# First phase of a packed-attention mixer: keys turned by TensorE, scores and packed values in small tiles

## The chip, the cores and the metric

The kernel runs on one core of one Trainium2 chip. The metric is the device time of one execution in microseconds. A core has five engines that run side by side, each strictly in the order of its own instructions: TensorE (PE, matrix products and turns by a product with the identity), VectorE (DVE), ScalarE (ACT), GpSimd (POOL) and SyncE (SP), which issues all the transfers of this kernel. They wait for each other by semaphores. Data lie in the SBUF memory with 128 partitions; TensorE writes into PSUM, which has eight banks of 512 fp32 columns; ACT and DVE bring results from there into SBUF.

## What is computed

Two attentions follow one another, then a mixer over tokens and channels. q, k and v are 8 x 8 x 576 x 64 (batch, head, token, head dimension), p is 8 x 8 x 32 x 64.

```python
def sm_attn(qq, kk, vv):
    s = scale * np.matmul(qq, kk.transpose(0, 1, 3, 2))
    s = s - np.max(s, axis=-1, keepdims=True)
    a = np.exp(s)
    a = a / (np.sum(a, axis=-1, keepdims=True) + 1e-09)
    return np.matmul(a, vv)
p_packed = sm_attn(p, k, v)
out = sm_attn(q, p_packed, p_packed)
...
xt = x.transpose(0, 2, 1)
h = xt @ U @ V
u = x + h.transpose(0, 2, 1)
ch = np.maximum(u @ w_ch1, 0.0) @ w_ch2
return (u + ch).astype(np.float32)
```

x is the attention's output with its heads side by side, 8 x 576 x 512. U, V, w_ch1 (512 x 2048) and w_ch2 (2048 x 512) come as 64-bit floats, and the kernel makes fp32 of their bits. Because the packed attention's result has only 32 rows a head, the kernel multiplies p_packed with w_ch1 first ("pp w1" below, the folds) and uses that product as weights later.

## The kernel before

**First phase (the loop `for i in range(NU + 3)`, lines 479 to 508).** A unit is one batch and four of its heads; there are 16. For each unit the keys come as rows (`load_nat`, line 97: 18 tokens of one head to a partition, 4.6 KB in one run), DVE turns them by 32x32 blocks into `kT` (`transposed`, line 101). p is scaled by GpSimd and turned by DVE into block-diagonal tiles `bdp` (lines 310 and 313). The scores of four heads are four fp32 products of 128x128 by 288 columns into one tile `s_ps` of two PSUM banks (line 322). Softmax takes a maximum on DVE (line 330) and an exponential with running sum on ACT (line 332). The weights are turned back by TensorE (lines 342 and 343; ACT copies them out at 345 and 346), and the packed values are five products of all four heads at once (lines 358 and 359), 256 columns wide, of which each head's 32 rows use their own 64 columns; ACT scales these four blocks into `ppall` (line 362). Values come as two transfers a unit (lines 300 and 302).

Beside it in the same loop: conversions of w1 from 64-bit bits (`some_w1`: ACT line 67, four DVE instructions at 68 to 71, a split by ACT 123 and GpSimd 124), the folds (`fold`: three products a piece at 76 to 78 into `w_ps`, copied out at 390 or 392, stored to `wsr`), the pairs (`a_pairs`) and the steps of `attention(0)`, 16 small functions, one popped in each turn from i = 5.

The order of the first phase is not written out by hand: a planner simulates the engines in time, with the program's order as priority, and fixes each engine's order and each buffer's reuse. The eight PSUM banks in this phase are two for `psT` (tag t), two for `s_ps`, one for `pp_ps` and three for `w_ps`.

**The large loop** (from the first `h_ps` product at lines 76 to 78 on) runs over 8 batches with 16 pieces each, in an order written out by hand (`manual_schedule`). It needs the packed result of the first batch's attention, the folds of the first two batches and the first pieces of w2.

Of the kernel before, what the change touches and what calls it, by code (L numbers as in the profile page):

```python
# [19 lines left out]
def packed_attention_mixer_kernel(  # L20
# [36 lines left out]
    HALF = ((0, 256), (256, 320))  # L57

# [71 lines left out]
    def load_uv(pool):  # L130
        bits = pool.tile([P, NB * D], F32, name="nat", bufs=3)
# [5 lines left out]
        vbits = pool.tile([P, NB * D], F32, name="nat", bufs=3).bitcast(I32)  # L137
# [143 lines left out]
    bdp = [sA.tile([P, 4, P], F32, name=f"bdp{i}", tag=f"bdp{i}", bufs=1) for i in range(2)]  # L281
# [4 lines left out]
    ua = {}  # L286

    def a_load(u):
        b, g = UN[u]
        ua[u] = {}  # L290
        if g == 0:
            ua[u]["p"] = sA.tile([P, 2, D], F32, name="pn")
            nc.sync.dma_start(out=ua[u]["p"], in_=p[b].rearrange("(g h) n d -> (h n) g d", g=2))
        ua[u]["nat"] = load_nat(sA, 3, k, b, g)

    def a_load_v(u):
        b, g = UN[u]
        gh = slice(4 * g, 4 * g + 4)
        vt = pipe.tile([P, 5, 4 * D], F32, name="vt", tag="vt", bufs=2)
        nc.sync.dma_start(out=vt[:, :4].rearrange("p h x -> p (h x)").rearrange("p (h x) -> p h x", h=4),  # L300
                          in_=v[b, gh, :SM].rearrange("h (p k) d -> p h (k d)", k=4))
        nc.sync.dma_start(out=vt[:64, 4].rearrange("p (h d) -> p h d", h=4),
                          in_=v[b, gh, SM:].rearrange("h p d -> p h d"))
        ua[u]["v"] = vt

    def a_split(u):
        b, g = UN[u]
        if g == 0:
            pn = ua[u]["p"]
            nc.gpsimd.tensor_scalar_mul(pn, pn, scale)  # L310
            for h in range(4):
                hs = slice(32 * h, 32 * h + 32)
                nc.vector.transpose(bdp[b % 2][hs, :, hs], pn[hs].rearrange("p g (e l) -> p (g e) l", l=32))  # L313
        ua[u]["kT"] = transposed(sA.tile([P, 2, S], F32, name="kT"), ua[u]["nat"])

    def a_scores(u):
        b, g = UN[u]
        kT = ua[u]["kT"]
        s_ps = psA.tile([P, 2, 512], F32, name="s_ps", bufs=1)
        for hf in range(2):  # L320
            for dh in range(2):
                nc.tensor.matmul(s_ps[:, hf, :288], lhsT=bdp[b % 2][:, 2 * g + dh], rhs=kT[:, dh, 288 * hf:288 * hf + 288],  # L322
                                 start=dh == 0, stop=dh == 1)
        ua[u]["s"] = s_ps

    def a_softmax(u):
        s = ua[u]["s"][:, :, :288]
        mx = sA.tile([P, 1], F32, name="mx")
        sm = sA.tile([P, 1], F32, name="sm", bufs=3)
        nc.vector.tensor_reduce(mx, s, axis=AX.XY, op=ALU.max, negate=True)  # L330
        e1 = sA.tile([P, 2, 288], F32, name="e1")
        nc.scalar.activation(e1, s, AF.Exp, bias=mx, accum_out=sm)
        ua[u]["e"] = e1.rearrange("p a x -> p (a x)")
        ua[u]["sum"] = sm

    def a_turn(u):
        e1 = ua[u]["e"]
        t_ps = psT.tile([P, 4, P], F32, name="t_ps", tag="t")
        t2_ps = psT.tile([P, 512], F32, name="t2_ps", tag="t")
        e1c = e1[:, :SM].rearrange("p (j k) -> p k j", k=4)  # L340
        for kk in range(4):
            nc.tensor.transpose(t_ps[:, kk], e1c[:, kk], ident)
        nc.tensor.transpose(t2_ps[:64, :P], e1[:, SM:], ident)
        eT = sA.tile([P, 5, P], F32, name="eT", bufs=2)
        nc.scalar.copy(eT[:, :4], t_ps)
        nc.scalar.copy(eT[:64, 4], t2_ps[:64, :P])
        ua[u]["eT"] = eT
        sm = ua[u]["sum"]
        nc.vector.tensor_scalar_add(sm, sm, 1e-9)
        nc.vector.reciprocal(sm, sm)  # L350

    def a_pack(u):
        b, g = UN[u]
        eT, vt, rs = ua[u]["eT"], ua[u]["v"], ua[u]["sum"]
        pp_ps = psA.tile([P, 4, D], F32, name="pp_ps", bufs=1)
        vm = vt[:, :4].rearrange("p h x -> p (h x)").rearrange("p (h k d) -> p k h d", h=4, k=4)
        for kk in range(4):
            nc.tensor.matmul(pp_ps, lhsT=eT[:, kk], rhs=vm[:, kk], start=kk == 0, stop=False)
        nc.tensor.matmul(pp_ps, lhsT=eT[:64, 4], rhs=vt[:64, 4].rearrange("p (h d) -> p h d", h=4), start=False, stop=True)
        for h in range(4):  # L360
            hs = slice(32 * h, 32 * h + 32)
            nc.scalar.activation(ppall[hs, b, g], pp_ps[hs, h], AF.Copy, scale=rs[hs])
        if b < B // 2:
            ua[u]["twice"] = sA.tile([P, 2, D], F32, name="twice", bufs=1)
            nc.scalar.copy(ua[u]["twice"], ppall[:, b, g].unsqueeze(1).to_broadcast([P, 2, D]))
# [91 lines left out]
    for t in bdp:  # L457
        nc.gpsimd.memset(t, 0.0)
# [326 lines left out]
```

## Time and profile before

| what | value |
|---|---|
| time, three runs: median (lowest to highest) | 871.32 us (870.49 to 874.37) |
| profiled execution, its own time | 876.01 us |
| its span in the trace | 874.2 us |
| TensorE busy in the span | 826.7 us (95%) |
| VectorE | 512.6 us (59%) |
| ScalarE | 374.0 us (43%) |
| GpSimd | 258.6 us (30%) |

The trace shows one execution. TensorE's busy time counts products that lie over one another in the pipeline as busy until their modelled end, so a full stretch isn't necessarily at peak. fp32 products show as two records each, those in fp32r as one. The granted clock is the share of its full speed that TensorE had.

### The profile page before, as it was taken

What the parts mean: (1) busy time and instruction counts of PE and PEld (TensorE: products, weight loads), DVE (VectorE), ACT (ScalarE), POOL (GpSimd) and SP (SyncE); (2) the same over time, 40 slices, a digit from 0 to 9 for tenths busy, and PEclk for the clock granted to TensorE, in tenths of its full rate; (3) what the DMA queues carried; (4) which work ended last, traced back from release to release, by engine and by line L of the source; (5) the groups of instructions that cost most, each with busy time, mean ns of one, the idle gap of its engine ahead of it and who ended that gap; (6) DMA issues with size and microseconds to landing.
All of it is one profiled execution on the core that took longest, in us unless ns stands there. A gap on an engine that the chain in (4) does not pass through costs nothing.

```text
span 874.2 us, 12574 instructions
## 1 busy us (share of the span) xinstructions
PE 826.7 (95%) x4440; PEld 706.8 (81%) x4440; DVE 512.6 (59%) x1032; ACT 374.0 (43%) x960; POOL 258.6 (30%) x230
## 2 busy tenths in 40 slices
PE   4779889988989999999999999999999999999997
PEld 2557666777879888888888888988888889889886
DVE  7999985889857876478676433443543424432220
ACT  2557576534445554455554332233333322333220
POOL 3302353545343313132233232323242313221110
PEclk9989997999999999999999999999999999999999
DMA  9869775723424444334453103010301120002001
GB/s 318 236 204 330 221 222 187 253 85 121 160 64 123 140 144 130 98 112 126 117 182 85 53 13 112 25 60 17 112 25 63 56 70 25 25 14 95 25 1 60
DMA packets 59998, 98.55 MB, mean 113 GB/s; under 512 B 12192, under 2 KB 36768, under 8 KB 59936
## 3 DMA queue, kind: packets, MB, share of 16 engines
q1 hardware_dynamic: 59936, 97.75, 36.0%
q8 instruction: 35, 0.57, 0.3%
q14 instruction: 27, 0.22, 0.1%
HBM read 71.52 MB, written 26.21 MB: 112 GB/s over the span
## 4 chain that ended last, share of the span: by engine, by line
PE 73%; DVE 17%; DMA 4%; ACT 3%; issue 3%; SPq 0%; POOL 0%; DVEq 0%; ACTq 0%; POOLq 0%
PE o L78 14%; PE o L77 14%; PE o L76 14%; PE h_ps L76 7%; PE h_ps L77 7%; PE h_ps L78 7%; DVE kT L101 3%; DVE os L70 2%; DVE natT L101 2%; DVE os L69 2%; DMA bits<-in_moe_w_ch_dram 2%; PE w_ps L592 2%; DVE os L71 2%; DVE os L68 2%; PE s_ps L322 2%
## 5 line engine op out<-in xcount | busy, mean ns | idle before, releaser
L640 DVE SCALAR_TENSOR_TENSOR hl<-h_ps,hh 128x256 fp32r<-128x256 f32 x256 | 104.1, 418 | 181.1 <-ACT hh L638 145.7
L78 PE MATMUL o<-w2h,hl 128*128 128x512 f32 x512 | 202.1, 395 | 0.0
L76 PE MATMUL o<-w2h,hh 128*128 128x512 f32 x512 | 201.3, 393 | 0.0
L77 PE MATMUL o<-w2l,hh 128*128 128x512 f32 x512 | 200.9, 392 | 0.0
L638 ACT ACTIVATE hh<-h_ps 128x256 fp32r<-128x256 f32 x256 | 96.0, 383 | 234.4 <-PE h_ps L78 231.4
L76 PE MATMUL h_ps<-ah,fold 128*128 128x256 f32 x496 | 149.3, 301 | 6.3 <-DVE hl L640 5.9
L453 POOL TENSOR_TENSOR fold<-fold 128x512 fp32r<-128x512 f32 x62 | 81.2, 1310 | 230.1 <-ACT fold L452 222.6
L77 PE MATMUL h_ps<-al,fold 128*128 128x256 f32 x496 | 146.1, 295 | 0.0
L78 PE MATMUL h_ps<-ah,fold 128*128 128x256 f32 x496 | 145.7, 294 | 0.0
L78 PEld LDWEIGHTS o<-w2h,hl 128*128 128x128 f32 x512 | 96.4, 188 | 21.6
L77 PEld LDWEIGHTS o<-w2l,hh 128*128 128x128 f32 x512 | 96.6, 189 | 17.5
L76 PEld LDWEIGHTS o<-w2h,hh 128*128 128x128 f32 x512 | 96.7, 189 | 16.8
L76 PEld LDWEIGHTS h_ps<-ah,fold 128*128 128x128 f32 x496 | 93.5, 188 | 13.4 <-DVE hl L640 10.3
L77 PEld LDWEIGHTS h_ps<-al,fold 128*128 128x128 f32 x496 | 93.5, 189 | 2.1
L78 PEld LDWEIGHTS h_ps<-ah,fold 128*128 128x128 f32 x496 | 93.3, 188 | 0.0
L181 POOL TENSOR_TENSOR nlo<-natT,nhi 128x576 fp32r<-128x576 f32 x32 | 46.0, 1453 | 115.5 <-ACT nhi L180 115.5
L68 DVE TENSOR_SCALAR os<-os 128x512 f32<-128x512 f32 (+2 forms) x51 | 37.1, 727 | 40.0 <-ACT os L67 39.9
L322 PE MATMUL s_ps<-kT,bdp 128*128 128x288 f32 x128 | 39.3, 457 | 9.4 <-DVE bdp L313 9.2
L180 ACT CAST nhi<-natT 128x576 fp32r<-128x576 f32 x32 | 20.7, 675 | 55.8 <-DVE natT L101 48.6
L124 POOL TENSOR_TENSOR w1l<-os,w1h 128x512 fp32r<-128x512 f32 x16 | 21.4, 1337 | 67.7 <-ACT w1h L123 61.1
L101 DVE STREAM_TRANSPOSE kT<-nat 128x1152 f32<-128x1152 f32 x16 | 37.3, 2329 | 5.7 <-DMA nat<-in_k_dram 5.6
L67 ACT ACTIVATE os<-bits 128x512 f32<-128x512 f32 x48 | 32.3, 674 | 18.9 <-DMA bits<-in_moe_w_ch_dram 14.7
(143 smaller groups left out, 1398.5 us busy)
## 6 DMA issues: line engine op xcount, KB each, us to landing
bits<-in_moe_w_ch_dram SPq DMA_DIRECT2D x48, 512.0 KB, 4.3
nat<-in_k_dram SPq DMA_DIRECT2D x16, 576.0 KB, 5.3
nat<-in_q_dram SPq DMA_DIRECT2D x16, 576.0 KB, 4.4
vt<-in_v_dram SPq DMA_DIRECT2D x16, 512.0 KB, 5.6
wsr<-fold SPq DMA_DIRECT2D x32, 256.0 KB, 3.8
out_dram<-bits SPq DMA_DIRECT2D x16, 512.0 KB, 3.0
wsc<-bits SPq DMA_DIRECT2D x64, 128.0 KB, 2.2
fold<-wsc SPq DMA_DIRECT2D x32, 256.0 KB, 2.8
```

The costliest lines, as they stand in the source:

```text
L67: nc.scalar.activation(t, high.bitcast(F32), AF.Abs)
L68: nc.vector.tensor_single_scalar(t, t, LEAST, op=ALU.max)
L76: nc.tensor.matmul(ps, lhsT=lh, rhs=rh, start=start, stop=False)
L77: nc.tensor.matmul(ps, lhsT=lh, rhs=rl, start=False, stop=False)
L78: nc.tensor.matmul(ps, lhsT=ll, rhs=rh, start=False, stop=stop)
L101: nc.vector.transpose(t.rearrange("p h (i c) -> p c h i", c=NB), nat.rearrange("p (c h l) -> p c h l", h=2, l=32),)
L124: nc.gpsimd.tensor_tensor(lo, x, hi.bitcast(F32), op=ALU.subtract)
L181: nc.gpsimd.tensor_tensor(lo[:, dh], t, hi[:, dh].bitcast(F32), op=ALU.subtract)
L322: nc.tensor.matmul(s_ps[:, hf, :288], lhsT=bdp[b % 2][:, 2 * g + dh], rhs=kT[:, dh, 288 * hf:288 * hf + 288], start=dh == 0, stop=dh == 1)
L453: nc.gpsimd.tensor_tensor(lo, raw, hi.bitcast(F32), op=ALU.subtract)
L638: nc.scalar.activation(hi, src, AF.Relu)
L640: nc.vector.scalar_tensor_tensor(lo, src, 0.0, hi.bitcast(F32), op0=ALU.max, op1=ALU.subtract)
```

## The change

Only the first phase is changed. Keys are loaded with nine tokens to a partition (two runs of 2.3 KB, two heads side by side), turned by TensorE in blocks of two tokens and copied out of PSUM by ACT and DVE, so that the head dimension of even tokens lies in partitions 0 to 63 and that of odd ones in 64 to 127. p is loaded twice side by side and turned by TensorE. The scores are eight products a unit with 64 rows and 32 columns of the array, into two banks, one for each half of the tokens. Softmax works on the two halves. Packed values are 20 products a unit with 32 columns of the array and 64 columns of data, without the blocks that were computed and not used; one ACT instruction scales them. Values come in five transfers a unit. The six PSUM banks of the phase are now three pairs, with tags k (turned keys, p, weights turned back and packed values), s and w. In the loop, w1's conversions and the steps of `attention(0)` come earlier, the latter two in a turn.

```diff
+    NT = 9
+    I = S // NT
+    KHALF = (slice(0, 5 * I), slice(5 * I, S))
+    KLAST = slice(4 * I, 5 * I)
...
-    psA = actx.enter_context(tc.tile_pool(name="psA", bufs=1, space=PSUM, reuse_waits="tile"))
+    psA = actx.enter_context(tc.tile_pool(name="psA", bufs=2, space=PSUM, reuse_waits="tile"))
...
+    def bank(tag):
+        return psA.tile([P, 512], F32, name=f"{tag}_ps", tag=tag)
...
+            pn[b] = sA.tile([P, 2, 2, D], F32, name="pn", bufs=1)
+            for z in range(2):
+                nc.sync.dma_start(out=pn[b][:, :, z], in_=p[b].rearrange("(g h) n d -> (h n) g d", g=2))
+        ua[u]["x"] = sA.tile([P, 2 * S], F32, name="kx", bufs=3)
+        nc.sync.dma_start(
+            out=ua[u]["x"].rearrange("p (h y) -> p h y", h=2),
+            in_=k[b, 4 * g:4 * g + 4].rearrange("(h z) (i c) d -> (z i) h (c d)", z=2, c=NT))
...
+        for h in range(4):
+            nc.sync.dma_start(out=vt[:, h], in_=main[h].rearrange("i (a x) -> i a x", a=2))
+        nc.sync.dma_start(out=vt[:64, 4].rearrange("p (h d) -> p h d", h=4), in_=rows[:, 8])
+
+    def a_p(b):
+        t_ps = bank("k")
+        pT[b] = sA.tile([P, 2, P], F32, name="pT")
+        for i in range(2):
+            nc.tensor.transpose(t_ps[:, P * i:P * i + P], pn[b][:, i].rearrange("p z d -> p (z d)"), ident)
+        nc.scalar.activation(pT[b].rearrange("p g n -> p (g n)"), t_ps[:, :2 * P], AF.Copy, scale=scale)
+
+    def a_turn(u):
...
+        t = ua[u]["t"] = sA.tile([P, 4, 5 * I], F32, name="kT")
+        x = ua[u]["x"].rearrange("p (h y) -> p h y", h=2)
+        for h in range(2):
+            t_ps = bank("k")
+            for j in range(4):
+                o = P * (2 * (j % 2) + j // 2)
+                nc.tensor.transpose(t_ps[:, o:o + P], x[:, h, P * j:P * j + P], ident)
+            src = t_ps.rearrange("p (k a z i) -> p a z k i", k=2, a=2, z=2)
+            for a in range(2):
+                dst = t[:, 2 * h:2 * h + 2, :4 * I].rearrange("p z (k i a) -> p z k i a", k=2, a=2)[:, :, :, :, a]
+                if a:
+                    nc.vector.tensor_copy(dst, src[:, a])
+                else:
+                    nc.scalar.copy(dst, src[:, a])
+        t_ps = bank("k")
+        for h in range(2):
+            nc.tensor.transpose(t_ps[:64, P * h:P * h + P], x[:, h, SM:], ident)
+        nc.scalar.copy(t[:64, :, KLAST], t_ps[:64, :2 * P].rearrange("p (h i) -> p h i", h=4))
+
+    def a_scores(u):
...
+        ss = [bank("s") for _ in range(2)]
+        for h in range(4):
+            hs = slice(32 * h, 32 * h + 32)
+            for r in range(2):
+                rs = slice(64 * r, 64 * r + 64)
+                n = KHALF[r].stop - KHALF[r].start
+                nc.tensor.matmul(ss[r][hs, :n], lhsT=lT[rs, g, hs], rhs=t[rs, h, :n], start=True, stop=True)
...
+        for r in range(2):
+            nc.vector.tensor_reduce(mx[:, r:r + 1], ss[r], axis=AX.X, op=ALU.max, negate=True)
+        nc.vector.tensor_tensor(mx[:, 2:], mx[:, :1], mx[:, 1:2], op=ALU.min)
+        e1 = ua[u]["e"] = sA.tile([P, S], F32, name="e1")
+        for r in range(2):
+            nc.scalar.activation(e1[:, KHALF[r]], ss[r], AF.Exp, bias=mx[:, 2:], accum_out=sm[:, r:r + 1])
+
+    def a_turn_back(u):
...
+        t_ps = bank("k")
+        for kk in range(4):
+            c0 = 5 * I * (kk % 2) + P * (kk // 2)
+            nc.tensor.transpose(t_ps[:, P * kk:P * kk + P], e1[:, c0:c0 + P], ident)
+        nc.scalar.copy(eT[:, :4].rearrange("p k x -> p (k x)"), t_ps)
+        t_ps = bank("k")
+        nc.tensor.transpose(t_ps[:64, :P], e1[:, KLAST], ident)
+        nc.vector.tensor_copy(eT[:64, 4], t_ps[:64, :P])
...
     def a_pack(u):
...
+        p_ps = bank("k")
+        vk = vt[:, :4].rearrange("p h x -> p (h x)").rearrange("p (h k d) -> p k h d", h=4, k=4)
+        for kk in range(5):
+            rows = P if kk < 4 else I
             for h in range(4):
                 hs = slice(32 * h, 32 * h + 32)
...
+                rhs = vk[:, kk, h] if kk < 4 else vt[:rows, 4, D * h:D * h + D]
+                nc.tensor.matmul(p_ps[hs, :D], lhsT=eT[:rows, kk, hs], rhs=rhs, start=kk == 0, stop=kk == 4)
         if b < B // 2:
...
+            nc.scalar.activation(ua[u]["twice"], p_ps[:, :D].unsqueeze(1).to_broadcast([P, 2, D]), AF.Copy, scale=ua[u]["rs"])
+            nc.gpsimd.tensor_copy(ppall[:, b, g], ua[u]["twice"][:, 0])
+        else:
+            nc.scalar.activation(ppall[:, b, g], p_ps[:, :D], AF.Copy, scale=ua[u]["rs"])
...
-            w_ps = psA.tile([P, 512], F32, name="w_ps", bufs=3)
+            w_ps = bank("w")
...
-            a_turn(i - 1)
+            a_turn_back(i - 1)
...
-        if i + 1 < NU:
-            a_split(i + 1)
+            a_turn(i + 1)
...
-        if i > 1:
+        if i > 0:
             some_w1()
...
-        if i >= 5 and first and i not in (16, 17):
-            first.pop(0)()
+        for _ in range(2):
+            if i >= 4 and first:
+                first.pop(0)()
...
-        if 6 < i < 13:
+        if 5 < i < 12:
             some_w1()
+        if i == 2:
+            uv = load_uv(sA)
         if i == 3:
-            uv = load_uv(sA)
-        if i == 4:
             prepare_uv(*uv)
```

More of the change, by code (lines that the diff above doesn't have):

```diff
@@ L130, in load_uv @@
     def load_uv(pool):
-        bits = pool.tile([P, NB * D], F32, name="nat", bufs=3)
+        bits = pool.tile([P, NB * D], F32, name="kx", bufs=3)
         ub = bits[:, :10 * R].bitcast(I32)
@@ new lines, in a_scores @@
+    def a_scores(u):
+        b, g = UN[u]
+        t, lT = ua[u]["t"], pT[b]
+        ss = [bank("s") for _ in range(2)]
[5 more added lines that the diff above has]
+                nc.tensor.matmul(ss[r][hs, :n], lhsT=lT[rs, g, hs], rhs=t[rs, h, :n], start=True, stop=True)
+        ua[u]["s"] = [ss[r][:, :KHALF[r].stop - KHALF[r].start] for r in range(2)]
@@ L316, in a_scores @@
[L316 to L350, printed above, removed]
```

53 lines of the change are left out of this document (20 added, 33 removed).

## The prediction

> **What bounds the kernel now.** I read three views first: the table of busy time by stretch, the engines' timeline for the ends of the first phase, and the chain of waits of that phase. The first timeline rows are the first scores, the last scores and the first product of the large loop.
>
> ```profile
> 9.16 4.18 PE L322 MATMUL s_ps<-kT,bdp 128*128 128x288 f32 x8 [9.16 <-DVE bdp L313]
> ...
> 120.72 2.11 PE L322 MATMUL s_ps<-kT,bdp 128*128 128x288 f32 x8
> ...
> 162.62 0.28 PE L76 MATMUL h_ps<-ah,wt 128*128 128x256 f32 x1
> ```
>
> The first phase therefore ends at 162.6 us: 9.2 us of start, then 16 units at a pace of (120.7 - 9.2) / 15 = 7.4 us, then 42 us from the last scores to the large loop. What follows it, 874.2 - 162.6 = 711.6 us, holds none of the changed code, and I leave it as it is. The question is only where the 162.6 goes.
>
> ```profile
> core 0: us, PE busy (x) PEld busy (x) DVE busy (x) ACT busy (x) POOL busy (x), PEclk, DMA share, GB/s
> 0.00:20.00 20.00, 8.40 (x29) 6.05 (x29) 14.11 (x22) 5.35 (x9) 8.42 (x18) 1.00 0.93 310
> 20.00:40.00 20.00, 14.24 (x65) 10.14 (x63) 19.50 (x35) 11.30 (x31) 6.63 (x7) 1.00 0.81 241
> 40.00:60.00 20.00, 14.60 (x47) 10.46 (x46) 18.76 (x42) 9.39 (x26) 1.16 (x2) 0.74 0.69 211
> 60.00:80.00 20.00, 19.88 (x91) 15.25 (x91) 19.09 (x34) 14.55 (x40) 4.34 (x4) 1.00 0.95 299
> 80.00:100.00 20.00, 17.64 (x80) 12.98 (x79) 19.50 (x32) 13.49 (x37) 6.83 (x5) 1.00 0.83 268
> 100.00:120.00 20.00, 18.14 (x78) 13.48 (x76) 18.64 (x37) 12.68 (x31) 7.54 (x6) 0.91 0.71 213
> 120.00:140.00 20.00, 16.59 (x60) 11.94 (x60) 11.66 (x22) 14.11 (x34) 9.46 (x7) 0.75 0.65 204
> 140.00:160.00 20.00, 17.45 (x74) 11.85 (x74) 14.46 (x24) 12.55 (x27) 10.24 (x11) 0.99 0.70 218
> ```
>
> Three stages are to be seen. Up to 60 us **VectorE (DVE)** is full, 38.3 of the last 40 us, while TensorE (PE) idles. From 60 to 120 us **both** are nearly full: DVE 57.2 and PE 55.7 of 60 us. After 120 us neither is, and transfers and conversions follow one another. So a microsecond taken from DVE is worth a microsecond only up to 60 us; after that PE is right behind it, and this change moves work onto PE.
>
> The chain of waits prices PE's work by what really passes between instructions (the busy times of PE overlap). It is a stretch in which PE is never idle:
>
> ```profile
> 62.93 1.94 PE s_ps L322 x8
> 64.87 1.73 PE pp_ps L358 x8
> 66.60 0.47 PE t_ps L342 x4
> 67.07 0.63 PE pp_ps L359 x2
> 67.70 0.43 PE w_ps L76
> 68.13 0.23 PE w_ps L77
> ...
> 70.53 0.11 PE t_ps L343
> ```
>
> An fp32 product of the program is two passes in the trace (four calls, eight records in `s_ps`): 1.94 / 8 = 0.242 us for 288 columns, 0.84 ns a column and pass. A turn of a 128x128 block costs 0.117 us. The product with 64 rows costs 0.315 a pass against 0.216 for those with 128 rows, and the one after it 0.43 against 0.23: entering and leaving 64 rows cost some 0.2 us each. A unit now takes PE 1.94 + 1.73 + 0.63 + 0.47 + 0.11 + 0.2 = **5.1 us**.
>
> **The change part by part.** DVE first, by these groups of the first 165 us:
>
> ```profile
> L101 DVE STREAM_TRANSPOSE kT<-nat 128x1152 f32<-128x1152 f32 x16 | 37.3, 2329 | 5.7 <-DMA nat<-in_k_dram 5.6
> L390 DVE COPY fold<-w_ps 128x512 f32<-128x512 f32 x8 | 5.5, 683 | 2.3 <-DMA wsr<-fold 2.3
> L362 ACT ACTIVATE ppall<-pp_ps,sm 32x64 f32<-32x64 f32 x64 | 19.5, 304 | 7.8 <-PE pp_ps L359 7.1
> L330 DVE TENSOR_REDUCE mx<-s_ps 128x1 f32<-128x576 f32 x16 | 12.0, 747 | 0.3
> L332 ACT ACTIVATE e<-s_ps,mx 128x576 f32<-128x576 f32 x16 | 11.8, 739 | 12.1 <-DVE mx L330 11.9
> L313 DVE STREAM_TRANSPOSE bdp<-pn 32x128 f32<-32x128 f32 x32 | 9.5, 295 | 0.4
> L346 ACT COPY eT<-t_ps 64x128 f32<-64x128 f32 x16 | 4.1, 257 | 0.7 <-PE t_ps L343 0.7
> L349 DVE TENSOR_SCALAR sm<-sm 128x1 f32<-128x1 f32 x16 | 2.3, 144 | 0.6 <-ACT e L332 0.5
> L332 ACT ACTIVATION_READ_ACCUMULATOR e<-s_ps,mx 128x1 f32 x16 | 3.1, 193 | 0.0
> L239 ACT CAST ms<-m_ps 128x256 fp32r<-128x256 f32 x1 | 0.4, 365 | 0.0
> ```
>
> It loses the turn of the keys and the block transposes of p: 37.3 + 9.5 = 46.8 us. It gains, per unit, two copies of 128x256 out of PSUM (half of the 683 ns row and a little: 0.37 each), the small copy of the turned weights (0.26, as ScalarE (ACT) needs for it now), one more maximum and a minimum (about 0.2: one more start and a one-column instruction of 0.14). That is 16 x 1.2 = 19 us, so DVE drops by **27 us**, from 135.7 us over these eight stretches to 109. At the fullness of the first 120 us (109.6 of 120 busy, 91%) that is 120 us of time: DVE no longer sets the phase.
>
> ACT gains two copies of 128x256 and the last token's, 3 x 0.365, a share of p's turn 0.19, the split of the exponential (one more start and accumulator read, 0.35), and loses the small copy 0.26 and four scalings, 1.22, for one of 0.3. Net +0.5 us a unit, 7 us in all on an engine that is busy 93 of 160: hidden behind the others. GpSimd loses the scaling of p and gains eight small copies: off the path.
>
> PE is the uncertain term. Turning keys adds 10 turns of 0.117 and half of p's two: 1.3 us. The way back keeps its 0.58. Entering and leaving 64 rows now happens twice a unit (scores and the last tile of values), four times 0.2 = 0.8.
>
> The scores become 8 calls of two passes with 320 or 256 columns, 0.27 and 0.215 us a pass. Nothing in this trace shows what tiles of 64x32 or 128x32 do side by side. One end is strictly in turn: 4 x 2 x (0.27 + 0.215) = 3.9 us. The other end is all eight tiles together: 0.54. I take the nearest mechanism: the two passes of a call use one tile and must follow each other, and records start in order, so only the second pass of a call lies beside the first of the next. That gives half, 1.94 + 0.2 = **2.1 us**, about today's.
>
> The values become 20 calls, 40 passes of 64 columns, each 0.054 us and each with a weight load. In turn at the streaming rate: 2.15. In pairs: 1.1. All four tiles of a column together: 0.54. If each pass costs the 0.11 us that the closest records of small products have now: 4.4. I take **1.6**, midway between pairs and in turn, since 40 loads must also get through. A unit: 1.3 + 2.1 + 0.6 + 1.6 + 0.8 = **6.4 us** against 5.1. The rest of PE's work in the phase is 96 passes of the folds at 0.23 = 22 us and about 7 us of attention(0) and pairs: 29. New PE work 16 x 6.4 + 29 = 131 us. At the 94% that PE reaches from 60 to 100 us (37.5 of 40) this is 140 us, plus 9 us of start, plus 2 for the end: the large loop would start at **151 us**, 11.6 us earlier. The time for that lost at half clock (granted 0.74 and 0.75 in two stretches) goes with PE's idle gaps, and I count no gain beyond.
>
> The Trainium skill, "TensorE: Matmul & The Clock Gate", Part 3, says that tiles in distinct row and column groups run beside each other, the later ones starting some 4 ns apart. No run here shows it. By it the scores and values would cost about 0.6 us each, which is the first rival below. "TensorEngine Tiling (Array Packing)", Key Properties, says that a change of the tiling mode drains TensorE. The 0.2 us at 64 rows agrees with it; the product with 64 columns, 0.11 us, shows no such price.
>
> The loads: k arrives as two runs a partition in place of one, p twice, v in five transfers in place of two.
>
> ```profile
> 120.14 0.38 SPq L300 DMA_DIRECT2D vt<-in_v_dram  x1
> 120.57 0.61 SPq L302 DMA_DIRECT2D vt<-in_v_dram  x1
> ...
> wsr<-fold SPq DMA_DIRECT2D x32, 256.0 KB, 3.8
> ```
>
> SyncE's (SP) issues grow by 3 x 0.38 + 0.2 for p, 1.3 us a unit of some 7: no bound. The bytes grow only by p's second copy, 0.5 MB at about 300 GB/s = 2 us spread over the phase. It shows only if the DMA share of 0.95 (60 to 80 us) holds everywhere.
>
> The moved steps are the conversions of w1 and the steps of attention(0), two a unit from unit 4. They add no work; they fill the stretch after the last scores (42 us now, with DVE 26 of 40 busy) earlier. That is what lets PE's sum set the phase at all; if they don't move, up to 10 us of the gain stays there.
>
> **The rivals.**
>
> 1. *Full overlap of tiles.* Scores 0.6 and values 0.6: a unit 3.9 us, PE 91 us in all. Then DVE's 120 us, 6 us of start and some 14 for the last folds, their store (3.8 us to land) and their reload decide: 140 us, 22 us gained, **849 us**. For it speaks that no two of the eight score tiles share rows and columns; against it that both passes of a call share one.
>
> 2. *Tiles in turn: PE becomes the bound, slower than before.* Place: scores and values. Price: 3.9 + 2.15 + 2.7 = 8.7 us a unit, 168 us of PE, 179 at 94%, 188 with the start: 25 us lost, **896 us**; with 0.11 a pass, 10.9 us a unit and about 935. It decides from the unit at which (16 x + 29) / 0.94 + 9 = 162.6: x = **7.2 us**. My 6.4 is not far from that. The stretch from 60 to 120 us, with PE at 93%, speaks for it.
>
> 3. *The two k banks.* Six and a half fills a unit (three for keys, two back, one for values, half for p) go through two banks. If the mean time from first write to last read is c, a unit needs 3.25 c; it decides from c = 7.4 / 3.25 = 2.3 us. Fill and eviction alone are 0.47 + 0.58, about 1.1, so 3.6 us a unit. But ACT now comes late: in one unit the bank was filled from 118.85 and its copy ended at 122.14, 3.3 us.
>
> ```profile
> 118.85 0.63 PE L342 MATMUL t_ps<-ident,e 128*128 128x128 f32 x4
> ...
> 121.57 0.57 ACT L345 COPY eT<-t_ps 128x512 f32<-128x512 f32 x1
> ```
>
> At 2.7 us, midway between 2.3 and that, the pace is 8.8 and the phase 15 x 1.4 = 21 us longer, less some 10 for the shorter end: 11 lost, **882 us**. Against it: other work (scores, folds, attention) has other banks and can stand between.
>
> 4. *Nothing gained.* PE units at 7 us, or the steps don't move forward: within 4 us, **871 us**.
>
> **How the numbers follow.** The profiled execution took 876.0 us, 1.8 outside its span; the median of three is 871.3. I set the gain against the median: 871.3 - 11.6 = 860, rounded up to **861** for p's bytes. Chances: forecast (a gain of 5 to 18) 0.37, full overlap 0.20, nothing gained 0.15, tiles in turn 0.15, k banks 0.13. About 0.5% (4.4 us) is what a measurement can tell: faster 0.57, same 0.15, slower 0.28. The range leaves one in ten on each side: from 838 (full overlap, with a shorter end too) to 892 (most of the way to tiles in turn). The likeliest case by itself is 853 to 867.
>
> **What would show it.** PE's timeline of one unit after: scores near 2.1 us and values near 1.6 confirm the pairs; 0.6 each, rival 1; 3.9 and 2.2 or more, rival 2. Groups: DVE down by 25 to 29 us in the first 150. Idle of PE before the key turns, released by ACT or DVE copies out of the k banks, beyond 1 us a unit shows rival 3. The first product of the large loop near 151 us. I am wrong if the part after it changes by more than 4 us, or if the first unit starts later than 12 us because of the added loads.

## The result, and the profile after

The kernel after took **897.2 us** (median of four runs, 896.12 to 899.77) against 872.85 us for the kernel before in the same session: **1.028 times as long [1.024, 1.032]**, so it is slower, outside the predicted range and on the other side. The forecast was 861.

The timeline of TensorE (start, duration, engine, line, operation, tiles) answers first. These are the first scores, one unit in the middle (values, then scores), the last scores and the first product of the large loop.

```profile
9.77 1.31 PE L361 MATMUL s_ps<-kT,pT 64*32 64x320 f32 x16
...
117.74 0.90 PE L400 MATMUL k_ps<-vt,eT 128*32 128x64 f32 x40
119.16 0.76 PE L361 MATMUL s_ps<-kT,pT 64*32 64x320 f32 x16
...
162.22 0.76 PE L361 MATMUL s_ps<-kT,pT 64*32 64x320 f32 x16
181.81 0.56 PE L82 MATMUL h_ps<-ah,wt 128*128 128x256 f32 x1
```

The large loop starts at 181.8 us in place of 162.6: 19.2 of the 21.6 us by which the span grew (895.8 against 874.2). What follows took 895.8 - 181.8 = 714.0 us against 711.6. Within the phase the pace is (162.2 - 9.8) / 15 = 10.2 us a unit in place of 7.4, while the stretch from the last scores to the loop shrank from 41.9 to 19.6 us. Yet TensorE's price of a unit fell far below the forecast: scores 0.76 us, values 0.90.

The table by stretch shows that no engine fills the phase as a whole any more; VectorE alone is full, and only from 40 to 80 us (37.2 of 40 us). After the first two columns (stretch, length) stand the busy times of TensorE, its weight loads, VectorE, ScalarE and GpSimd, then the granted clock.

```profile
core 0: us, PE busy (x) PEld busy (x) DVE busy (x) ACT busy (x) POOL busy (x), PEclk, DMA share, GB/s
0.00:20.00 20.00, 10.99 (x60) 5.38 (x61) 8.23 (x20) 7.88 (x17) 5.56 (x13) 1.00 0.85 275
20.00:40.00 20.00, 11.25 (x105) 6.00 (x104) 15.93 (x36) 9.05 (x25) 4.60 (x5) 0.72 0.75 252
40.00:60.00 20.00, 12.24 (x102) 7.63 (x106) 18.09 (x43) 10.91 (x31) 5.75 (x5) 0.50 0.65 193
60.00:80.00 20.00, 16.11 (x177) 10.58 (x169) 19.10 (x41) 12.62 (x30) 9.54 (x9) 0.93 0.83 250
80.00:100.00 20.00, 15.00 (x160) 9.40 (x160) 15.75 (x34) 14.23 (x37) 10.44 (x10) 0.83 0.96 306
100.00:120.00 20.00, 15.80 (x167) 8.96 (x168) 11.76 (x33) 13.54 (x37) 6.50 (x7) 0.91 0.82 233
120.00:140.00 20.00, 15.63 (x168) 10.50 (x169) 7.84 (x22) 9.28 (x25) 0.00 (x0) 0.78 0.97 281
140.00:160.00 20.00, 18.29 (x192) 12.76 (x192) 11.93 (x35) 11.79 (x37) 3.15 (x4) 0.96 0.44 131
```

VectorE's eight rows add up to 108.6 us, where 109 was forecast, but the phase isn't over at 160 us now. TensorE, which was to set the phase at 94%, is busy for 11 to 16 of 20 us in most rows. It waits, and one unit shows for what:

```profile
65.01 0.66 PE L338 MATMUL k_ps<-ident,kx 128*128 128x128 f32 x4 [0.34 <-DVE eT L385]
66.17 0.66 PE L338 MATMUL k_ps<-ident,kx 128*128 128x128 f32 x4 [0.50 <-ACT pT L325]
67.48 0.39 ACT L345 COPY kT<-k_ps 128x256 f32<-128x256 f32 x1
68.20 0.40 ACT L345 COPY kT<-k_ps 128x256 f32<-128x256 f32 x1
69.30 0.42 DVE L343 COPY kT<-k_ps 128x256 f32<-128x256 f32 x1
69.78 0.41 PE L348 MATMUL k_ps<-ident,kx 128*64 128x128 f32 x2 [1.04 <-DVE kT L343]
70.75 0.41 DVE L343 COPY kT<-k_ps 128x256 f32<-128x256 f32 x1
```

The first key bank is filled from 65.01; ScalarE copies its half out at 67.48, VectorE the other half only at 69.30. Both banks with tag k are taken by then, so the turn of the last token (L348) and everything behind it in TensorE's order stand until 69.78. The bank was held for 69.72 - 65.01 = 4.71 us, the second for 71.16 - 66.17 = 4.99.

In this unit no idle time stands before VectorE's copies: it is at other work when ScalarE's copy ends. But that it comes second is no chance. In all 32 banks of the trace its copy starts after ScalarE's of the same bank has ended, and the groups of the first 182 us (line, operation, count, busy, mean; idle time before them and what ended it) show it waiting for that in other units:

```profile
L338 PE MATMUL k_ps<-ident,kx 128*128 128x128 f32 x128 | 25.6, 345 | 12.2 <-ACT pT L325 6.7 <-DVE eT L385 4.0 <-DMA kx<-in_k_dram 1.2
L343 DVE COPY kT<-k_ps 128x256 f32<-128x256 f32 x32 | 13.3, 420 | 15.3 <-ACT kT L345 15.0
L345 ACT COPY kT<-k_ps 128x256 f32<-128x256 f32 x32 | 12.2, 393 | 6.9 <-PE k_ps L338 6.9
L348 PE MATMUL k_ps<-ident,kx 128*64 128x128 f32 x32 | 8.0, 342 | 9.5 <-DVE kT L343 8.8 <-DMA bits<-in_moe_w_ch_dram 0.4
```

VectorE idles 15.0 us for ScalarE's copies, TensorE 8.8 us for VectorE's and 10.7 for other copies out of the same two banks (`pT`, `eT`). Over the 32 banks, from the start of the first of the four turns to the end of the later copy, a bank is held for **3.40 us** on average; in units 4 to 9 (counted from 0), 12 banks turned between 41 and 104 us, for 4.54. Of the 4.54 us the turns take 0.81, the wait until ScalarE comes 2.03, its copy 0.40, the wait until VectorE comes 0.89 and its copy 0.42. VectorE is idle for only 0.04 of its 0.89: there a bank waits in two busy queues, one after the other.

### The profile page after: what moved, and what is told of

Read it like the earlier page. It is cut to its first block, busy times and chain, and to the rows that moved or that the text cites. A ratio compares the mean times of both kernels' runs of the same rounds, so it can differ in the third digit from the quotient of the medians.

```text
span 895.8 us, 14249 instructions
## 1 busy us (share of the span) xinstructions
PE 826.0 (92%) x5224; PEld 694.2 (77%) x5224; DVE 493.1 (55%) x1064; ACT 376.1 (42%) x976; POOL 255.1 (28%) x228
## 4 chain that ended last, share of the span: by engine, by line
PE 74%; DVE 8%; ACT 3%; DMA 3%; issue 2%; POOL 1%; SPq 1%; ACTq 0%; DVEq 0%
PE o L82 14%; PE o L84 14%; PE o L83 14%; PE h_ps L82 7%; PE h_ps L83 7%; PE h_ps L84 7%; PE w_ps L631 2%; DVE os L75 2%; DMA bits<-in_moe_w_ch_dram 1%; PE m_ps L242 1%; DVE os L74 1%; DVE natT L107 1%; DVE os L76 1%; DVE os L77 1%; PE t_ps L231 1%
## 5 line engine op out<-in xcount | busy, mean ns | idle before, releaser
L258 POOL TENSOR_TENSOR al<-aT,ah 128x288 fp32r<-128x288 f32 x32 | 25.2, 810 | 69.8 <-ACT ah L257 69.8
L75 DVE TENSOR_SCALAR os<-os 128x512 int32<-128x512 int32 (+2 forms) x51 | 37.5, 735 | 9.7 <-POOL wt L494 7.9
L73 ACT ACTIVATE os<-bits 128x512 f32<-128x512 f32 x48 | 32.4, 674 | 22.8 <-DMA bits<-in_moe_w_ch_dram 12.6
L493 ACT CAST fold<-fold 128x512 fp32r<-128x512 f32 x62 | 38.8, 626 | 0.2
```

Source lines behind the costliest of these rows:

```text
L73: nc.scalar.activation(t, high.bitcast(F32), AF.Abs)
L75: nc.vector.tensor_scalar(x, t.bitcast(I32), 3, 0x3FFFFFF8, op0=ALU.logical_shift_left, op1=ALU.bitwise_and)
L258: nc.gpsimd.tensor_tensor(al[:, g, ns], aT[:, ns], ah[:, g, ns].bitcast(F32), op=ALU.subtract)
L493: nc.scalar.copy(hi, raw)
```

## The experiments

Two theories stood at the start. **A**: two k banks, each emptied by two copies in series, set the pace. **B**: the moved steps and added transfers fill the queues. Every time below is the median of the runs of that kernel; the ratio is to the kernel before, run beside it (873.4 to 874.4 us). "Loop" is the start of the large loop.

**The loop as it was.**

```diff
-        if i > 0:
+        if i > 1:
             some_w1()
...
-        for _ in range(2):
-            if i >= 4 and first:
-                first.pop(0)()
+        if i >= 5 and first and i not in (16, 17):
+            first.pop(0)()
```

The second call of `some_w1` and the loads of U and V go back to their places too.

> The changed kernel with the loop of before: w1's conversions from the third turn on and one extra from 7 to 12, one step of attention(0) a turn from i = 5, U and V loaded a turn later. Theory A (the two k banks and their copies set the pace of a unit, 10.2 us, whatever else stands in the queues): the last scores stay near 160 us, the steps of attention(0) come after them, and the time is 895 to 905 us. Theory B (the moved steps fill ACT and DVE ahead of the copies and take both vt buffers of the value loads in the middle of the units): the pace falls to 8 us or less, the last scores come before 135 us, the kernel takes 870 to 885 us.

Measured 900.33 us, 1.030 [1.025, 1.035], the last scores at 160.9, loop at 186.3: theory A. The moved steps are not the loss.

**One engine a bank.** Each bank is emptied by one engine, with the same four copies of the same size:

```diff
-                if a:
+                if h:
                     nc.vector.tensor_copy(dst, src[:, a])
```

> The changed kernel, but the two copies out of a k bank of turned keys are made by one engine (first bank ACT, second DVE) instead of one by each. In the changed kernel the DVE copy always starts after the ACT copy of the same bank has ended (DVE idle 15 us for it). Theory A (the copies in series hold the bank): that idle time goes, PE waits less for kT copies (22 us now), the pace falls by 1 to 1.5 us a unit and the time by 10 to 20 us. Theory B (queues filled by moved steps): the wait moves into the queue of the one engine, and the time stays within 5 us of 897.

Measured **881.65 us**, 1.009 [1.006, 1.012], loop at 161.74: 15.6 us of time, and 20 us of phase in the profiled run (878.51 us, the lowest of six), from one line. The timeline of this kernel shows the two banks emptied side by side:

```profile
99.57 1.09 PE L338 MATMUL k_ps<-ident,kx 128*128 128x128 f32 x8
101.57 0.66 ACT L345 COPY kT<-k_ps 128x256 f32<-128x256 f32 x2
101.65 0.76 DVE L343 COPY kT<-k_ps 128x256 f32<-128x256 f32 x2
102.28 0.41 PE L348 MATMUL k_ps<-ident,kx 128*64 128x128 f32 x2 [0.41 <-ACT kT L345]
```

and its groups (first 162 us) no wait of one copy for the other:

```profile
L343 DVE COPY kT<-k_ps 128x256 f32<-128x256 f32 x32 | 12.0, 418 | 9.8 <-PE k_ps L338 9.6
L348 PE MATMUL k_ps<-ident,kx 128*64 128x128 f32 x32 | 7.4, 321 | 2.9 <-ACT kT L345 2.5 <-DVE kT L343 0.2
```

A bank is held for 2.34 us on average, and for 2.57 in the 12 banks of units 4 to 9: the wait for the first copy is 1.03 us there, and the second copy follows in the same queue. In these units the arithmetic nearly closes: 1.97 us less a bank, two such fills a unit through two banks, is 2.0 us a unit. From unit 3's scores to unit 9's the pace is (97.50 - 35.15) / 6 = 10.4 us here, (110.00 - 34.31) / 6 = 12.6 in the kernel after: 2.2 us. In these units TensorE was at half clock for 38 of 76 us in the kernel after and for 30 of 62 here, about half of the time in both. The last six units don't follow that sum: they gain 6.7 us (45.5 against 52.2) with a bank held only 0.2 us less, but the kernel after has 11 us at half clock there and this one none.

**Three k banks** (the folds keep one bank with tag w).

```diff
-tag=tag)
+tag=tag, bufs={"k": 3, "s": 2, "w": 1}[tag])
```

> The changed kernel with three k banks and one w bank instead of two and two. Theory A: a third bank takes a third off the ring's price, PE's idle time before key turns, values and turns back falls from some 40 us to 20, the time falls by 10 us or more in spite of folds that now wait for their one bank (32 folds, each up to 1 us longer, beside other work). Theory B: no more than 5 us.

Measured 891.07 us, 1.019 [1.013, 1.025]: 6 us better, between the two theories. The units did get faster, with the last scores at 126.1 us, but the loop starts at 174.8. The folds, with one bank, come last; the rows by stretch show that they also run at half clock:

```profile
140.00:160.00 20.00, 14.91 (x31) 8.20 (x31) 6.97 (x12) 6.08 (x11) 6.71 (x11) 0.50 0.59 205
```

Only 31 products in 20 us. So the pace was taken back and then lost again elsewhere.

**Only the packed values in small tiles, in the kernel before.** Its 20 products of 32 columns replace the five wide ones, and one ACT scaling the four; nothing else is changed.

```diff
+            for h in range(4):
+                rhs = vm[:, kk, h] if kk < 4 else vt[:rows, 4, D * h:D * h + D]
+                nc.tensor.matmul(pp_ps[hs, 0], lhsT=eT[:rows, kk, hs], rhs=rhs, start=kk == 0, stop=kk == 4)
...
+        nc.scalar.activation(ppall[:, b, g], pp_ps[:, 0], AF.Copy, scale=rs)
```

> The kernel before with one part of the change alone: packed values in 20 products of 128x32 (64 columns each) and one scaling by ACT in place of four; keys, scores, banks, loads and loop as before. From the changed kernel's rows the values cost 0.83 us a unit there against 2.36 plus 0.2 before: 27 us off PE and 15 us off ACT. Theory A and B both leave this part out of the blame: it gains. DVE stays full until 60 us and PE falls behind it from 60 to 120: I expect 5 to 15 us gained, 858 to 867 us. If small tiles themselves cost (clock, drains), it is no faster than before.

Measured 878.57 us, 1.006 [1.003, 1.008]: the gain of 5 to 15 us didn't come, and the kernel is no faster than before. The products are as cheap as in the kernel after:

```profile
99.93 0.65 PE L362 MATMUL pp_ps<-vt,eT 128*32 128x64 f32 x32
102.65 0.32 PE L362 MATMUL pp_ps<-vt,eT 64*32 64x64 f32 x8
```

0.97 us for what took 2.36, and the last scores come 7.4 us earlier (113.3). But the loop starts 3.3 us later, at 165.9: after the scores TensorE waits for conversions and for banks of the folds, and has half of its clock from 134.7 to 158.6 us. The row of that stretch, and some of its folds:

```profile
140.00:160.00 20.00, 13.30 (x34) 9.06 (x34) 12.58 (x17) 8.79 (x16) 9.57 (x10) 0.54 0.65 202
```

```profile
153.20 0.80 PE L76 MATMUL w_ps<-w1h,lwh 128*128 128x512 f32 x1 [3.32 <-DVE fold L391]
153.79 0.63 PE L77 MATMUL w_ps<-w1l,lwh 128*128 128x512 f32 x1
154.22 0.63 PE L78 MATMUL w_ps<-w1h,lwl 128*128 128x512 f32 x1
154.64 0.63 PE L76 MATMUL w_ps<-w1h,lwh 128*128 128x512 f32 x1
```

One fold product follows the other after 0.43 us, where the prediction counts 0.23. What TensorE gained in the units came back as idle time and half clock.

**Is it the place of the copies, or the bank?** The copies of a bank interleave token by token. This kernel lets each engine take one half of the columns, and so removes the interleaving, with the order of all instructions on TensorE, GpSimd and SyncE unchanged.

```diff
-            src = t_ps.rearrange("p (k a z i) -> p a z k i", k=2, a=2, z=2)
+            src = t_ps.rearrange("p (k a z i) -> p k a z i", k=2, a=2, z=2)
...
-                if a:
-                    nc.vector.tensor_copy(dst, src[:, a])
+                if kh:
+                    nc.vector.tensor_copy(dst, src[:, kh])
```

> The kernel after, with one edit: VectorE's and ScalarE's copies of a bank of turned keys each take one half of its columns (k = 0 and k = 1) instead of every other token (a = 0 and a = 1), so their sources and destinations no longer interleave. Work, instructions and sizes stay. Theory C1, VectorE waits for ScalarE because the two copies' places interleave: then the two copies start within 0.1 us of one another in most units, the first product of the large loop comes at 160 us (156 to 166; 181.8 in the kernel after, 161.7 with one engine a bank), 876 to 884 us. Theory C2, it waits because both copies read one bank: VectorE's copy still starts only when ScalarE's has ended, 181.8 +- 4 us, 893 to 901 us.

Measured 896.64 us, 1.025 [1.022, 1.028], loop at 178.6. The copies still follow one another, in all 32 banks:

```profile
113.70 0.40 ACT L345 COPY kT<-k_ps 128x256 f32<-128x256 f32 x1 [0.74 <-PE k_ps L338]
114.16 0.42 DVE L343 COPY kT<-k_ps 128x256 f32<-128x256 f32 x1
116.41 0.39 ACT L345 COPY kT<-k_ps 128x256 f32<-128x256 f32 x1
116.83 0.42 DVE L343 COPY kT<-k_ps 128x256 f32<-128x256 f32 x1 [1.99 <-ACT kT L345]
```

Disjoint columns don't help, so theory C2 holds: sharing one bank is what orders them. The common destination `kT` is not: with one engine a bank both engines write it too, side by side. A tile of tag k is a whole bank, so these runs don't tell whether the program orders by tile or by bank. The Trainium skill, "PSUM — Partial Sum Buffer", section "PSUM bank collisions raise a hardware error", says that two different engines may not access one bank in the same 32 partitions at once, two readers included and disjoint columns too, and that software has to order them. The order seen in all these banks agrees; no run here leaves it out.

**Other versions with one engine a bank.** The first takes back only the order of attention(0) (the second hunk of the first experiment's diff), the second adds a third k bank, the third has the old loop.

> The kernel after with one engine a bank, and the steps of attention(0) as before, one a unit from unit 5. In the run with one engine a bank the loads of v waited on SyncE from 113.8 to 125.7 us for a vt buffer that attention(0)'s tokens held. Theory B' (this is what is left of the loss against the kernel before): without it the last scores come at 130 to 140 us (143 there), the large loop starts at 150 to 157 us, 869 to 877 us. Theory A' (the stall lies beside other work, PE's chain of turns and copies sets the pace anyway): last scores 140 to 147, 161 +- 4 us, 878 to 885 us.

892.83 us, 1.020 [1.016, 1.023]; neither theory. The last scores come at 157.1. In this kernel a load of w2 stands on SyncE for 14.1 us behind `aT` of attention(0), a wait that the kernel with one engine a bank doesn't have. Changing one step changes the planner's order on every engine, and with it which waits come up.

> One engine a bank and three k banks (the folds keep one w bank). Theory A' (two k banks still set the pace): last scores at 120 to 128 us (143 with two banks and one engine a bank, 126 with three banks and two engines a bank), then a tail as long as that of the run with three banks, 45 to 49 us, large loop at 165 to 175, 881 to 891 us. Theory B' (the v loads set it): last scores stay at 138 or later, large loop at 165 or later.

896.88 us, 1.025 [1.021, 1.029]. Last scores at 118.5, as theory A' expects, then 59 us to the loop at 177.9, so that the time is above its range. In this tail VectorE's and ScalarE's copies of folds wait 20.5 and 21.9 us for products, and the granted clock is 0.50 from 160 to 180 us.

> One engine a bank and the old order of the loop (w1's conversions, attention(0) and U, V a unit later, one step of attention a unit). Theory A': the moved steps matter little, as they did with the serial copies (897.2 and 900.3 us): 878 to 886 us, large loop at 158 to 168. Theory B': with the copies out of the way the steps in SyncE's and ScalarE's queues are next: 869 to 877 us, large loop at 150 to 157.

**875.81 us**, 1.002 [1.000, 1.004], the best version of this study: within 0.5% of the kernel before. The time lies in the range of theory B', the loop in that of A': in the profiled run, the slowest of ten (879.99 us), it starts at 165.0, no earlier than with one engine a bank alone (161.74). So neither is shown.

**The two engines exchanged** (`if not h:`), to see how much hangs on one order of the planner.

> As the run with one engine a bank (881.65 us), with the two engines exchanged: VectorE copies bank 0 of a unit's keys and ScalarE bank 1. Work, waits by kind and sizes are the same; the order that the planner lays out differs on PE in 402 lines. Theory A (the serial copies were the cause): 877 to 886 us. Rival P (the planner's order of the first phase decides, and one engine a bank only happened on a good one): anywhere between 875 and 900, outside 877 to 886 if it is large.

879.45 us, 1.006 [1.004, 1.008], loop at 161.8: theory A. One of the ten runs took 4408 us; nothing on record says why, and the ratio rests on the other nine (877.4 to 881.3).

**v in three transfers.** The tokens of a chunk are ordered so that the two halves of the partitions load v for all four heads at once; the copies stay on two engines.

```diff
-        for h in range(4):
-            nc.sync.dma_start(out=vt[:, h], in_=main[h].rearrange("i (a x) -> i a x", a=2))
+        for a in range(2):
+            nc.sync.dma_start(out=vt[64 * a:64 * a + 64, :4], in_=main[:, :, 4 * D * a:4 * D * a + 4 * D])
```

> The kernel after with the tokens of a chunk ordered (a, i) in place of (i, a): the copies out of the k banks write runs of 64 elements, and v comes in three transfers a unit in place of five, 1.2 us of SyncE's issue less. The copies of one bank stay on two engines. Theory A: no change beyond 5 us, 890 to 900 us. Theory B (SyncE's queue with the added transfers sets the pace): half of the loss or more comes back, 874 to 886 us.

897.47 us, 1.028 [1.023, 1.032], loop at 177.3: theory A. The same with one engine a bank:

> One engine a bank and v in three transfers, the loop as in the kernel after. If SyncE's issue of v is what is left beside the serial copies (loads of v landed at 150 to 154 us in the run with one engine a bank): 870 to 877 us, large loop at 150 to 158. If not: 878 to 886.

877.20 us, 1.004 [1.001, 1.007], loop at 162.4. The interval touches that of the kernel with five transfers (1.006 to 1.012), so a gain isn't settled.

> One engine a bank, the old order of the loop, v in three transfers: a candidate to beat both kernels. If SyncE's issue still binds: 866 to 872 us, large loop at 152 to 158 (165.0 without it). If not: 873 to 879, as the run without it (875.81).

886.65 us, 1.014 [1.010, 1.018], 11 us worse than without the three transfers: a miss. Between 84 and 125 us its units are 12 to 17 us apart, and from 80 to 173 us TensorE waits 11.3 us for the small `eT` copy.

**Four banks in common for turned keys and folds.** This gives turned keys more banks without leaving the folds one.

```diff
-tag=tag)
+tag="s" if tag == "s" else "k", bufs=2 if tag == "s" else 4)
```

> The kernel after with the folds' banks and the k banks as four banks in common (2 + 2 before); the two copies of a bank stay on two engines. Theory A (serial copies cost because two banks must hold 6.5 fills a unit): with more banks the wait lies beside other turns, last scores at 110 to 135 us, large loop at 155 to 170, 873 to 886 us. If the wait itself, in the order of PE's or VectorE's work, is the price whatever the banks: 890 to 900.

890.17 us, 1.018 [1.016, 1.020], loop at 172.5. The copies remain in series and a bank is still held for 2.94 us, but TensorE's turn of the last token no longer waits for them (8.8 us in the kernel after):

```profile
L343 DVE COPY kT<-k_ps 128x256 f32<-128x256 f32 x32 | 13.1, 417 | 10.2 <-ACT kT L345 10.0
L348 PE MATMUL k_ps<-ident,kx 128*64 128x128 f32 x32 | 7.3, 316 | 0.0
```

The time lies at the bottom of the range of "the wait itself": the units are as fast as theory A says until 96 us, then come up to 22 us apart. So A is right about where the wait was paid, and wrong about what it is worth in this setting.

> One engine a bank and four banks in common. If banks are still the bound with one engine a bank: 866 to 875 us, large loop at 150 to 158. If something else is: 876 to 884.

894.00 us, 1.022 [1.020, 1.025], loop at 179.7: above both ranges. With four banks one engine a bank gains nothing. From 60 to 180 us TensorE now waits elsewhere, at folds whose banks ScalarE still has to empty of turned keys:

```profile
PE w_ps L82 <- ACT kT L345: 7.4, 2, 4.6
```

> As before it, with v in three transfers a unit. If banks and SyncE's issue were what is left: 862 to 870 us. If not, as the run with one engine a bank and v in three transfers (877.2): 873 to 881.

889.32 us, 1.016 [1.014, 1.019], again above both ranges.

> One engine a bank, four banks in common and the old order of the loop. Against the same with two k banks (875.81): 866 to 872 if banks were left as the bound, 873 to 880 if not.

888.10 us, 1.015 [1.013, 1.017], above both ranges too.

**The folds' stores on GpSimd's queue.** In the kernel of four common banks with one engine a bank, loads of v for the last units stood behind seven stores of folds on SyncE:

```profile
133.19 11.68 SPq L434 DMA_DIRECT2D wsr<-fold  x7
...
145.30 2.52 SPq L317 DMA_DIRECT2D vt<-in_v_dram  x4
```

```diff
-            nc.sync.dma_start(out=wsr[r][P * pr:P * pr + P, cs], in_=st)
+            nc.gpsimd.dma_start(out=wsr[r][P * pr:P * pr + P, cs], in_=st)
```

> One engine a bank, four banks in common, v in three transfers (889.3 us), and the folds' stores issued by GpSimd in place of SyncE. If the loads behind the stores hold the last units back: last scores at 115 to 135 us (152.7 without), large loop at 155 to 162, 868 to 880 us. If not (the conversions of w1 that stand ahead of the folds on PE do): 884 to 893 us.

889.29 us, 1.018 [1.015, 1.020], the last scores at 152.3 as without the edit (152.7). The stores are not it.

> One engine a bank, two k banks, v in three transfers (877.2 us), and the folds' stores issued by GpSimd: a candidate to beat both kernels. If SyncE's queue is what is left: 864 to 872 us, large loop at 148 to 157 (162.4 without). If not: 873 to 881 us.

879.33 us, 1.007 [1.004, 1.009], loop at 163.6: no gain.

**What the runs say together.** The kernels that differ only in who empties a bank, in us:

| banks | loop, transfers of v | two engines a bank | one engine a bank | difference |
|---|---|---|---|---|
| k 2, w 2 | new, 5 | 897.2 | 881.65 (exchanged 879.45) | -15.6 (-17.8) |
| k 2, w 2 | old, 5 | 900.33 | 875.81 | -24.5 |
| k 2, w 2 | new, 3 | 897.47 | 877.20 | -20.3 |
| k 3, w 1 | new, 5 | 891.07 | 896.88 | +5.8 |
| 4 in common | new, 5 | 890.17 | 894.00 | +3.8 |

With two k banks the serial copies cost 15.6 to 24.5 us in each of three settings. All seven kernels with two k banks and one engine a bank (875.8 to 892.8 us) are faster than all four with two engines (896.6 to 900.3). With more banks no cost shows. That fits a price paid through the banks that the copies hold. What remains open is what keeps the kernels with more banks at 888 to 897 us, and those with two k banks and one engine a bank at no less than 876. The stores of folds, SyncE's transfers of v and the old loop were tried; none brought a kernel below the one before. Two kernels with one engine a bank (892.83 and 886.65) show that one small edit can cost some 11 us, most likely through the planner's order, so a difference of that size between two single kernels proves little here. No version beat the kernel before.

One rival to the plain account is left open in part. The time that TensorE's granted clock stands at 0.50 in the first 190 us of each trace goes with the result: 27 us in the kernel before; 44 to 61 us in the five kernels with two k banks and one engine a bank at 876 to 882 us, and in the one with only the values in small tiles; 68 to 85 us in those at 888 to 900 us. (The traces of the kernels at 886.65 and 897.47 us are left aside: their records of the clock begin only at 36 and 46 us.) 44 us more at half clock, as from before to after, are up to 22 us of TensorE's full-speed work. The sums over the first phase, of the kernel before, the one after and the one with one engine a bank, show what grew:

```profile
0.00:162.62 162.62, 129.56 (x524) 93.99 (x525) 137.12 (x244) 94.03 (x235) 56.38 (x64) 0.93 0.79 247
0.00:181.81 181.81, 125.96 (x1309) 77.84 (x1309) 118.92 (x277) 96.07 (x251) 52.28 (x62) 0.81 0.76 233
0.00:161.74 161.74, 117.46 (x1309) 73.92 (x1309) 116.89 (x277) 95.25 (x251) 51.34 (x62) 0.84 0.84 260
```

TensorE's idle time, the stretch less its busy time, is 33.1, 55.9 and 44.3 us. From before to after it grows by 22.8 us, more than the phase does. One engine a bank takes back 11.6 us of idle and 8.5 us of busy time, the latter with at least 15 us less at half clock in the phase. And the units can be as slow without more half clock. These are the ten units from unit 5's scores to the last, in the kernel before and in the one with two engines a bank and v in three transfers (897.47 us), whose clock is on record there:

```profile
45.80:120.72 74.92, 66.05 (x282) 49.36 (x280) 70.99 (x130) 47.11 (x124) 19.95 (x16) 0.93 0.78 243
53.03:157.61 104.58, 77.55 (x865) 49.99 (x864) 76.17 (x173) 64.49 (x170) 34.70 (x31) 0.93 0.90 251
```

At the same granted clock of 0.93 they take 30 us longer. So the clock alone doesn't make the loss. Longer waits may still cost twice, once themselves and once through the clock, and a slow clock also makes the phase longer and so lengthens itself. No run holds the clock fixed, so how the whole loss divides is not settled.

## Why the prediction was wrong

- **VectorE down by 27 us: too much.** The first 160 us have the forecast's sum, 108.6 against 109, only because the phase isn't over there. Over the whole phase VectorE falls from 137.1 to 118.9 us, 18 less, and in the first 150 us by 23.8, where 25 to 29 were to confirm it. The added copies, maximum and minimum take 24 us where 19 were counted (the minimum 0.31 us for 0.14). It was right that VectorE then no longer sets the phase as a whole, though it is full again from 40 to 80 us.
- **TensorE's unit of 6.4 us: mis-sized, to the good side.** Scores 0.76 us where 2.1 was taken, values 0.90 where 1.6 was: near the first rival's price, full overlap (0.6 each). The Trainium skill's rule of "TensorE: Matmul & The Clock Gate", Part 3, that tiles in distinct row and column groups run beside each other, agrees with these rows in kind, and the 0.6 us worked out from it is short by 0.16 and 0.30. The reason given against it, that both passes of a call share a tile, doesn't hold: 16 score passes of up to 320 columns, 3.9 us in turn, took 0.76. That TensorE's busy time in the phase, 126.0 us, still lies near the forecast's sum of 131 is luck: the tiles saved about 2 us a unit, and 68 us of the phase were at half clock.
- **"That is what lets PE's sum set the phase": the step that failed.** The forecast's 151 us leave TensorE 20 us idle beside its 131 us of work (9 for the start, 9 at 94%, 2 for the end). It was idle for 55.9 of 181.8. ScalarE's new work was counted as hidden, VectorE as no longer setting the phase, and nothing was asked of the order of the two copies out of one bank. They run one after the other, each in its place in a busy engine's order, while the bank is held. No wait was priced for that; with one engine a bank the idle time falls to 44.3 us and the loop starts 20 us earlier.
- **The third rival, the two k banks: right in mechanism, wrong in size and given 0.13.** Its sign for "what would show it" is there: idle time of TensorE before the turns of keys, ended by copies out of k banks, is 8.8 + 6.7 + 4.0 = 19.5 us, or 1.2 us a unit where it asked for 1. It took 2.7 us for a bank's mean time (midway between its 2.3 and 3.3 is 2.8). Over all 104 fills, from the first write to the end of the last copy out, 2.50 was measured: 3.40 for turned keys, 2.10 for the others. So its formula gives 3.25 x 2.50 = 8.1 us a unit, above the 7.4 of before, and 10.2 was measured. With one engine a bank it gives 3.25 x 2.18 = 7.1, and 8.9 was measured. The banks also stand empty between fills, so the formula is a lower bound, and the rest of the pace is other waits and work. From the first scores to the last 41 us were lost (152.5 against 111.6), where the rival had 21; the gain at the end was 22.3 us (41.9 - 19.6), not some 10; the first scores came 0.6 later. Together that is the +19.2 us at the loop.
- **The moved steps: right that they shorten the end, wrong that it helps.** The old loop has 25.5 us from the last scores to the large loop, the new one 19.6, so 6 of the 22 us are theirs. With serial copies the old loop is no better (900.33); with one engine a bank the old loop is at least as good (875.81 against 881.65).
- **The loads: no bound, right.** Three transfers in place of five changed nothing in the kernel after (897.47). The first unit came at 9.8 us, and the rest after the phase changed by 2.4 us, within the 4 allowed.
- **Rival 2, tiles in turn: refuted**, with a unit's scores and values at 1.7 us against its 6. The loss has the size that it forecast (896 us) for another reason.

## What to carry to other kernels

In this program two engines that empty one PSUM bank do so one after the other, whatever columns they read: give each engine a bank of its own when banks are few. Before counting busy time, count fills times holding time over the number of banks, as a lower bound. Making an engine lighter gained nothing here, because the work then waited: look for the buffer whose release comes last, and price its whole stay, the place of the copy in its engine's queue included. Where a planner fixes the order, test a cause in several settings, because one edit moves others by as much as the effect.

## What was unexpected in the hardware

- Small tiles overlap well even for fp32 calls of two passes each: 16 passes of 320 and 256 columns with 64 rows and 32 columns in 0.76 us, 40 passes of 64 columns in 0.90 (at half clock 1.31 and 1.45).
- Half clock came in stretches where TensorE was busy for part of the time only: from 28.9 to 63.0 us in the kernel after, with 11 to 12 of 20 us busy, and for 44 us from 133.1 with three k banks, with 15 of 20. Every kernel of this study has more of it than the kernel before.
- The first scores of the kernel after took 1.31 us, as at half clock, in a stretch whose row says 1.00. The trace has no record of the granted clock before 22 us there, so that the durations tell more than the row.
